# Loading the second chunk of w1 on ScalarE's DMA queue, and SyncE's loads in the order of the source

## The chip, the cores and the metric

The kernel runs on one core of one Trainium2 chip. The metric is device time in microseconds (us), the median of several executions of the same program. The engines are TensorE (PE; its weight loads are shown apart, as PEld), VectorE (DVE), ScalarE (ACT), GpSimd (POOL) and SyncE (SP). SP only issues DMAs; its queue is shown as SPq, that of ScalarE as ACTq.

## The reference, cut to what matters

Two branches are computed from the same input x (2048 rows of 448) and mixed with a gate of one number per row: a linear-attention block (A) and a two-layer network with a squared ReLU (B).

```python
x = A_x
g = _sigmoid((x * gate_w).sum(-1, keepdims=True))
a = _A_ref(x, A_wqkv, A_wo)              # linear attention, 16 heads
h = x @ w1 + b1                          # 448 -> 1792
r = where(h > 0, h, 0);  h = r * r
b = h @ w2 + b2                          # 1792 -> 448
return g * a + (1 - g) * b
```

The change touches only how the first pieces of x and w1 come into SBUF.

## The kernel before

All matmuls run on operands that are split into a high and a low part, so that three products of a pair (high by high, high by low, low by high) give the accuracy of 32 bits. `split_hi` writes the high part (on ACT, here), `split_lo` the low part, source minus high part, on DVE. The 448 columns of the contraction are cut into four chunks c = 0 to 3 of 128 rows (the last holds 64 columns twice). x is cut into four blocks of 512 rows; a chunk of a block is a tile of 128 by 512, 256 KB. w1 is cut into two halves h of 896 columns, each half into a part g = 0 of 512 and a part g = 1 of 384 columns.

The kernel begins with 14 small matmuls on a constant (line 177, tile `warm_ps`). Meanwhile SP issues the first loads. Chunk 0 of x and of w1 come together in two loads, `xwr`, each with half of the columns of both. Then come, in pairs, chunks 1, 2 and 3 of x (`xr`) and of w1 (`w1r`, from `in_w1a`), then b1, two tiles of w2, four of wk and the g = 1 part of w1. The loop over c at line 549 works on four groups of 128 columns of w1 (f = 0 to 3) at once, in four PSUM banks. For c = 0 it splits the two `xwr` tiles and multiplies the high parts in four matmuls of 256 columns (line 549), then come ten matmuls of 512 columns (line 229). For c = 1 and 2, ACT writes x's high part (`xh<-xr`) and w1's (`w<-w1r`), DVE x's low part (`xl<-xr,xh`) and w1's (`w<-w1r,w`), each in this order, and PE does twelve matmuls: for each f, w high by x high, w high by x low, w low by x high. For c = 3 there are eight. Then PE goes on to the keys (`k_ps`) and the second layer (`o_ps`).

The order on PE, ACT and DVE is that of the source: these three engines stand in the set that `manual_schedule` names (line 170). SP's order was up to a scheduler. A load into a tile of `work` waits until the tile that had its place is read; there are 15 places (`NSLOT`). Besides, the loads share eight completion semaphores in turn, so that one that takes a semaphore waits until the load that had it before has landed. `half` is a table of 128 by 2 that the queries of the last phase use.

Of the kernel before, what the change touches and what calls it, by code (L numbers as in the profile page):

```python
# [7 lines left out]
F = mybir.dt.float32  # L8
R = mybir.dt.float32r
AF = mybir.ActivationFunctionType  # L10
# [5 lines left out]
P = 128  # L16
# [14 lines left out]
def gated_mix_kernel(ctx: ExitStack, tc: tile.TileContext, xw, xt, xn, wk, wq, wv, wo, w1a, w1b, w2, b1, b2, gw,  # L31
                     hmask, kvmask, halves, out):
    nc = tc.nc
    act, dve, pool, pe, sp = nc.scalar, nc.vector, nc.gpsimd, nc.tensor, nc.sync
# [19 lines left out]
    def slot(shape, dt, name):  # L54
        return work.tile(shape, dt, name=name, tag="s", bufs=NSLOT)

    def load(dst, src):
        sp.dma_start(out=dst, in_=src)
# [45 lines left out]
    def load_x(b, c):  # L104
        x_raw[b, c] = slot([P, TB], F, f"xr{b}_{c}")
        load(x_raw[b, c], xt[b, c])
# [21 lines left out]

    w1_s, w1_raw = {}, {}

    def load_w1(h, g, c):
        w1_raw[h, g, c] = slot([P, (TB, 3 * P)[g]], F, f"w1r{h}{g}{c}")
        load(w1_raw[h, g, c], (w1a, w1b)[g][h, c])

    def new_w1(h, g):
        n, a, z = ((TB, 0, 16), (3 * P, 48, 0))[g]
# [30 lines left out]
        load(wk_raw[c], wk[c])  # L167


    ctx.enter_context(tc.manual_schedule(engines={pe.engine, act.engine, dve.engine}))  # L170


    part = [keep.tile([P, D], F, name=f"part{t}") for t in range(NT)]
# [13 lines left out]
        load(xw_raw[n], xw[n])  # L187
    for c in range(1, 4):
        load_x(0, c)
        load_w1(0, 0, c)  # L190
    b1_s = keep.tile([P, NF], F, name="b1_s")
    half = keep.tile([P, 2], F, name="half")
    ones = keep.tile([P, 2], F, name="ones")
    logit = keep.tile([P, NT], F, name="logit")
# [7 lines left out]
    for c in range(4):  # L202
        load_w1(0, 1, c)
# [415 lines left out]
    for b in range(1, NB):  # L619
        for f in range(NH):  # L620
# [46 lines left out]
            if b == 3:  # L667
                if f < 4:
                    load_w1(1, 0, f)
                if f == 4:  # L670
                    for c in range(4):
                        split_w1(1, 0, c)
                if f >= 2:
                    load_w2(NH + f - 2)
                if f >= 3:
                    split_w2(NH + f - 3)
                if f == 5:
                    key_sums()
                if f >= 5:
                    load_kv(2 * f - 10)  # L680
                    load_kv(2 * f - 9)
# [151 lines left out]
```

## Time and profile before

| | us |
|---|---|
| median of 3 runs | 435.24 (435.14 to 435.32) |
| profiled execution, its own time | 435.1 |
| its span, first to last instruction | 433.3 |
| PE busy | 429.0 |
| DVE busy | 284.2 |
| ACT busy | 174.6 |
| POOL busy | 72.0 |

Times in the views below are microseconds from the start of the span. PE is busy nearly always; what can be won or lost is in the stretches in which its weight loads wait. A busy PE counts a matmul's time in the pipeline, so two matmuls in a row overlap, and the pace is read from start to start.

### The profile page before, as it was taken

What the parts mean: (1) busy time and instruction counts of PE and PEld (TensorE: products, weight loads), DVE (VectorE), ACT (ScalarE), POOL (GpSimd) and SP (SyncE); (2) the same over time, 40 slices, a digit from 0 to 9 for tenths busy, and PEclk for the clock granted to TensorE, in tenths of its full rate; (3) what the DMA queues carried; (4) which work ended last, traced back from release to release, by engine and by line L of the source; (5) the groups of instructions that cost most, each with busy time, mean ns of one, the idle gap of its engine ahead of it and who ended that gap; (6) DMA issues with size and microseconds to landing.
All of it is one profiled execution on the core that took longest, in us unless ns stands there. A gap on an engine that the chain in (4) does not pass through costs nothing.

```text
span 433.3 us, 5562 instructions
## 1 busy us (share of the span) xinstructions
PE 429.0 (99%) x2052; PEld 380.6 (88%) x2052; DVE 284.2 (66%) x463; ACT 174.6 (40%) x302; POOL 72.0 (17%) x93
## 2 busy tenths in 40 slices
PE   9999999999999999999999999999999999999996
PEld 6889999898989899898898888988888888888986
DVE  5999518843499437884459777877654967457624
ACT  6865324521346132453145543444433534233421
POOL 0045006500065002540010441000100001000000
PEclk9999999999999999999999999999999999999999
DMA  8741302020232211223244321230101401002002
GB/s 277 246 134 61 99 0 69 26 67 2 70 85 65 70 45 48 66 57 111 63 117 146 72 63 38 63 120 0 26 0 48 137 0 27 0 0 86 0 2 85
DMA packets 18411, 29.11 MB, mean 67 GB/s; under 512 B 2896, under 2 KB 12736, under 8 KB 18384
## 3 DMA queue, kind: packets, MB, share of 16 engines
q1 hardware_dynamic: 16480, 26.46, 19.6%
q0 software_dynamic: 1760, 2.20, 2.3%
q8 instruction: 16, 0.26, 0.3%
q10 hardware_dynamic: 144, 0.10, 0.1%
q14 instruction: 11, 0.09, 0.1%
HBM read 22.43 MB, written 3.67 MB: 60 GB/s over the span
## 4 chain that ended last, share of the span: by engine, by line
PE 98%; DMA 1%; DVE 0%; ACT 0%; DVEq 0%; issue 0%
PE h_ps L229 32%; PE o_ps L254 31%; PE q_ps L84 8%; PE a_ps L84 8%; PE g_ps L84 8%; PE k_ps L254 8%; PE kv_ps L405 1%; DMA xwr<-in_xw 1%; PE m_ps L84 1%; PE d_ps L84 0%; PE h_ps L549 0%; PE z_ps L399 0%; DVE out L278 0%; ACT xh L65 0%; DVEq L829 0%
## 5 line engine op out<-in xcount | busy, mean ns | idle before, releaser
L254 PE MATMUL o_ps<-w,hh 128*128 128x448 f32 x448 | 129.0, 362 | 0.0
L229 PE MATMUL h_ps<-xh,w 128*128 128x512 f32 x390 | 124.7, 390 | 0.0
L254 PEld LDWEIGHTS o_ps<-w,hh 128*128 128x128 f32 x448 | 84.0, 187 | 7.7
L229 PE MATMUL h_ps<-xl,w 128*128 128x512 f32 x224 | 86.7, 389 | 0.0
L229 PEld LDWEIGHTS h_ps<-xh,w 128*128 128x128 f32 x390 | 73.1, 188 | 14.8 <-DVE w L72 0.4
L254 PE MATMUL o_ps<-w,hl 128*128 128x448 f32 x224 | 81.2, 362 | 0.0
L233 ACT ACTIVATE hr<-h_ps,b_s 128x512 f32<-128x512 f32 x56 | 38.1, 680 | 85.9 <-PE h_ps L229 80.6
L69 DVE CAST hh<-hr 128x512 fp32r<-128x512 f32 x56 | 23.6, 421 | 61.4 <-ACT hr L234 61.3
L229 PEld LDWEIGHTS h_ps<-xl,w 128*128 128x128 f32 x224 | 42.0, 188 | 7.8
L254 PEld LDWEIGHTS o_ps<-w,hl 128*128 128x128 f32 x224 | 42.0, 188 | 3.7
L72 DVE TENSOR_TENSOR hl<-hr,hh 128x512 fp32r<-128x512 f32 x56 | 39.7, 709 | 3.3
L72 POOL TENSOR_TENSOR nl<-xnr,nh 128x384 fp32r<-128x384 f32 x16 | 17.2, 1075 | 119.0 <-ACT nh L65 118.9
L234 ACT ACTIVATE hr<-hr 128x512 f32<-128x512 f32 x56 | 35.4, 632 | 1.8
L84 PE MATMUL q_ps<-xh,wq_s 128*128 128x512 f32 x100 | 33.0, 389 | 0.0
L84 PE MATMUL a_ps<-m_s,qh 128*128 128x448 f32 x112 | 32.7, 362 | 0.0
L254 PE MATMUL k_ps<-wk_s,xh 128*128 128x448 f32 x112 | 32.7, 361 | 0.0
L476 POOL DMA_DIRECT2D qr<-qv x16 | 7.9, 500 | 124.3 <-ACT qv L473 94.4
L72 DVE TENSOR_TENSOR pl<-r,ph 128x448 fp32r<-128x448 f32 x16 | 23.7, 1480 | 0.0
L327 POOL TENSOR_TENSOR ksum<-ksum,r 128x448 f32<-128x448 f32 x15 | 23.3, 1555 | 1.1 <-DVE r L289 1.1
L84 PE MATMUL q_ps<-xl,wq_s 128*128 128x512 f32 x60 | 23.3, 389 | 0.0
L254 PE MATMUL k_ps<-wk_s,xl 128*128 128x448 f32 x64 | 23.2, 363 | 0.0
L84 PE MATMUL a_ps<-m_s,ql 128*128 128x448 f32 x64 | 23.2, 362 | 0.0
(112 smaller groups left out, 565.9 us busy)
## 6 DMA issues: line engine op xcount, KB each, us to landing
xr<-in_xt SPq DMA_DIRECT2D x27, 256.0 KB, 2.7
xnr<-in_xn SPq DMA_DIRECT2D x16, 224.0 KB, 2.5
out<-out SPq DMA_DIRECT2D x15, 224.0 KB, 1.9
w2r<-in_w SPq DMA_DIRECT2D x14, 224.0 KB, 2.8
w1r<-in_w1a SPq DMA_DIRECT2D x7, 256.0 KB, 2.8
w1r<-in_w1b SPq DMA_DIRECT2D x8, 192.0 KB, 3.3
m_s<-m POOLq DMA_DIRECT2D x12, 112.0 KB, 2.5
wqr<-in_wq SPq DMA_DIRECT2D x4, 256.0 KB, 2.6
```

What stands on the lines that cost most here:

```text
L69: eng.tensor_copy(hi, src)
L72: eng.tensor_tensor(lo, src, f32(hi), op=ALU.subtract)
L84: pe.matmul(out_ps, a, b, start=(i == 0), stop=(i == n - 1))
L229: pe.matmul(ps, a, m, start=(c == 0 and n == 0), stop=(c == 3 and n == 1))
L233: act.activation(r, ps, AF.Relu, bias=b1_s[:, f:f + 1])
L234: act.activation(r, r, AF.Square)
L254: pe.matmul(ps, a, m, start=start, stop=stop)
L327: pool.tensor_tensor(ksum, ksum, p, op=ALU.add)
L405: pe.matmul(kv_ps[:JE, js], wv_s[c][:, js], gsum[c][:, js], start=(c == 0), stop=(c == 3))
L476: pool.dma_start(out=r[p + 16:p + 32], in_=v[p:p + 16])
```

## The change

`load_w1` gets a queue as an argument. For chunk 1 of the first part of w1 it is ACT's: ACT first writes a constant into one column of the destination tile, and then issues the load, which has to come behind that write. The table of functions that ACT loads before its first activation thereby stands before the load. A second small activation writes a column of `b1_s`, so that SP's load of b1 has to come behind it. SP joins the engines whose order is the source's. The loads of x's chunk 1 and chunk 2 now follow each other on SP, and chunk 2 of w1 comes behind them. The load of `half` goes from behind b2 to the place that it has in the source.

```diff
-    def load_w1(h, g, c):
+    def load_w1(h, g, c, queue=sp):
         w1_raw[h, g, c] = slot([P, (TB, 3 * P)[g]], F, f"w1r{h}{g}{c}")
-        load(w1_raw[h, g, c], (w1a, w1b)[g][h, c])
+        if queue is act:
+            act.activation(w1_raw[h, g, c][:, :1], nc.const_aps.tensor(1.0, (P, 1), F), AF.Copy)
+        queue.dma_start(out=w1_raw[h, g, c], in_=(w1a, w1b)[g][h, c])
...
-    ctx.enter_context(tc.manual_schedule(engines={pe.engine, act.engine, dve.engine}))
+    ctx.enter_context(tc.manual_schedule(engines={pe.engine, act.engine, dve.engine, sp.engine}))
...
     for c in range(1, 4):
         load_x(0, c)
-        load_w1(0, 0, c)
+        if c > 1:
+            load_w1(0, 0, c)
+
+
     b1_s = keep.tile([P, NF], F, name="b1_s")
+    load_w1(0, 0, 1, act)
+    act.activation(b1_s[:, :1], nc.const_aps.tensor(1.0, (P, 1), F), AF.Copy)
```

SP at the program's start, before (`xr0_1` is chunk 1 of x's block 0, `w1r001` is chunk 1 of w1's half 0, part 0; the last number only counts tiles):

```order
L58 DMA xwr0_110<-in_xw 128x512
L58 DMA xwr1_112<-in_xw 128x512
L58 DMA xr0_1_114<-in_xt 128x512
L58 DMA w1r001_116<-in_w1a 128x512
L58 DMA xr0_2_118<-in_xt 128x512
L58 DMA w1r002_120<-in_w1a 128x512
L58 DMA xr0_3_122<-in_xt 128x512
L58 DMA w1r003_124<-in_w1a 128x512
L58 DMA b1_s_126<-in_b1 128x14
```

and after:

```order
L58 DMA xwr0_110<-in_xw 128x512
L58 DMA xwr1_112<-in_xw 128x512
L58 DMA xr0_1_114<-in_xt 128x512
L58 DMA xr0_2_116<-in_xt 128x512
L135 DMA w1r002_118<-in_w1a 128x512
L58 DMA xr0_3_120<-in_xt 128x512
L135 DMA w1r003_122<-in_w1a 128x512
L58 DMA b1_s_124<-in_b1 128x14
```

The load of `w1r001` has left SP's queue, and each load behind it stands one place earlier.

ACT at the program's start, before:

```order
L65 ACT_TABLE_LOAD
L65 ACTIVATE xh0_169<-xwr0_110 128x256
L65 ACTIVATE xh0_169<-xwr1_112 128x256
L65 ACTIVATE xh0_169<-xr0_1_114 128x512
L65 ACTIVATE w1_00_171<-w1r001_116 128x512
L65 ACTIVATE xh0_169<-xr0_2_118 128x512
```

and after:

```order
L134 ACT_TABLE_LOAD
L134 ACTIVATE w1r001_125<-const-float32-1.0 128x1
L135 DMA w1r001_125<-in_w1a 128x512
L198 ACTIVATE b1_s_124<-const-float32-1.0 128x1
L65 ACTIVATE xh0_171<-xwr0_110 128x256
L65 ACTIVATE xh0_171<-xwr1_112 128x256
L65 ACTIVATE xh0_171<-xr0_1_114 128x512
L65 ACTIVATE w1_00_173<-w1r001_125 128x512
L65 ACTIVATE xh0_171<-xr0_2_116 128x512
```

Three instructions stand between the table load and the first high part; the order of the high parts themselves is as before. On PE, DVE and POOL nothing has moved.

## Rows read from the trace of the kernel before

**Rows 1.** The page: span, and busy time of each engine.

```profile
span 433.3 us, 5562 instructions
...
PE 429.0 (99%) x2052; PEld 380.6 (88%) x2052; DVE 284.2 (66%) x463; ACT 174.6 (40%) x302; POOL 72.0 (17%) x93
```

**Rows 2.** Waits of weight loads, whole span: total us, times, longest.

```profile
PEld h_ps L549 <- ACT xh L65: 0.6, 1, 0.6
PEld h_ps L229 <- DVE w L72: 0.4, 1, 0.4
PEld h_ps L229 <- ACT w L65: 0.4, 1, 0.4
```

**Rows 3.** Timeline of PE's start, from several windows: start, us, instruction, count.

```profile
0.78 3.15 PE L177 MATMUL warm_ps<-const-bfloat16-1.0 128*128 128x256 bf16 x14 [0.78 <-PEq L825]
4.01 1.21 PE L549 MATMUL h_ps<-xh,w 128*128 128x256 f32 x4
...
4.63 0.59 PE L549 MATMUL h_ps<-xh,w 128*128 128x256 f32 x2
...
6.45 1.08 PE L229 MATMUL h_ps<-xh,w 128*128 128x512 f32 x4
...
8.77 0.40 PE L229 MATMUL h_ps<-xl,w 128*128 128x512 f32 x1
9.00 0.62 PE L229 MATMUL h_ps<-xh,w 128*128 128x512 f32 x2
...
9.69 0.62 PE L229 MATMUL h_ps<-xh,w 128*128 128x512 f32 x2
```

**Rows 4.** Timeline of weight loads, 6.9 to 9 us; in brackets, idle time before.

```profile
7.47 0.19 PEld L229 LDWEIGHTS h_ps<-xh,w 128*128 128x128 f32 x1 [0.36 <-ACT w L65]
...
8.19 0.30 PEld L229 LDWEIGHTS h_ps<-xh,w 128*128 128x128 f32 x2 [0.43 <-DVE w L72]
```

**Rows 5.** Timeline of ACT's start.

```profile
0.74 1.28 ACT L65 ACT_TABLE_LOAD   x1 [0.74 <-PEq L825]
...
4.16 0.42 ACT L65 ACTIVATE xh<-xwr 128x256 fp32r<-128x256 f32 x1 [0.20 <-DMA xwr<-in_xw]
5.87 0.63 ACT L65 ACTIVATE xh<-xr 128x512 fp32r<-128x512 f32 x1 [1.29 <-DMA xr<-in_xt]
6.78 0.63 ACT L65 ACTIVATE w<-w1r 128x512 fp32r<-128x512 f32 x1 [0.28 <-DMA w1r<-in_w1a]
7.46 0.63 ACT L65 ACTIVATE xh<-xr 128x512 fp32r<-128x512 f32 x1
...
13.99 0.69 ACT L233 ACTIVATE hr<-h_ps,b_s 128x512 f32<-128x512 f32 x1 [0.38 <-PE h_ps L229]
```

**Rows 6.** Timeline of DVE, 3 to 9 us.

```profile
6.54 0.69 DVE L72 TENSOR_TENSOR xl<-xr,xh 128x512 fp32r<-128x512 f32 x1 [0.74 <-ACT xh L65]
7.45 0.69 DVE L72 TENSOR_TENSOR w<-w1r,w 128x512 fp32r<-128x512 f32 x1 [0.22 <-ACT w L65]
```

**Rows 7.** Timeline of SP's start: when it issues a DMA, and how long.

```profile
0.74 0.86 SPq L58 DMA_DIRECT2D xwr<-in_xw  x2
1.64 0.43 SPq L58 DMA_DIRECT2D xr<-in_xt  x1
2.12 0.43 SPq L58 DMA_DIRECT2D w1r<-in_w1a  x1
```

**Rows 8.** DMA issues at 1.6 and 2.1 us: count, KB, us from issue to landing.

```profile
xr<-in_xt SPq DMA_DIRECT2D x1, 256.0 KB, 4.2
...
w1r<-in_w1a SPq DMA_DIRECT2D x1, 256.0 KB, 4.6
```

**Rows 9.** Windows: busy of PE, PEld, DVE, ACT, POOL; PEclk, DMA share, GB/s.

```profile
2.50:4.50 2.00, 1.91 (x9) 1.18 (x7) 0.64 (x3) 0.76 (x2) 0.00 (x0) 1.00 1.01 369
4.50:7.50 3.00, 3.00 (x15) 2.17 (x14) 2.04 (x6) 1.39 (x4) 0.00 (x0) 1.00 0.99 293
```

**Rows 10.** The smallest activation (by line), and `half`'s first reader (by tile).

```profile
L380 ACT ACTIVATE gate<-logit 128x16 f32<-128x16 f32 x1 | 0.2, 199 | 0.0
...
L77 ACT ACTIVATE ql<-qe,half x4: 723/724/726, 271.5 to 407.3; 128x512 fp32r<-128x512 f32 x4
```

## Prediction

> **What bounds the kernel now.** I first read the busy times on the page [rows 1]: PE is busy 429.0 of 433.3 us, so only its own waits, or its own pace, can move the end. Then the waits of its weight loads over the whole span [rows 2]: apart from 0.7 us before the first warm-up matmul there are three, 0.6, 0.4 and 0.4 us, and the timelines put all three ahead of 8.2 us [rows 3, 4]. After that the loads never starve PE. So the change, which moves only loads at the start, can at most remove what lies there, and a delay made there goes straight to the end, since nothing later is idle to take it up.
>
> The first wait (PE's first real matmul at 4.01) hangs on `xwr`, whose two issues the change leaves first on SP. The other two are chunk 1. The ten 512-column matmuls of chunk 0 end with four that start from 6.45 on [rows 3]. The pace of such matmuls without waits is 0.23 us: three start between 9.00 and 9.69. So the next was due at 6.45 + 4 x 0.23 = 7.37. It came at 7.47, released by ACT's high part of w1 [rows 4], and the third at 8.19, released by DVE's low part of w1. Behind each wait the next matmul comes 0.33 us later rather than 0.23. Follow it to the fifth matmul of chunk 1, which starts at 8.77 [rows 3] and would be due at 7.37 + 4 x 0.23 = 8.29: chunk 1 costs 0.48 us of waiting. **This is the most that the change can win.** 0.2% of this kernel, about what a measurement can tell from no change, is 0.87 us.
>
> **How chunk 1 comes to its times.** x's chunk 1 is issued at 1.64 and lands 4.2 us later, w1's at 2.12 and 4.6 us later [rows 7, 8], thus at 5.84 and 6.72. ACT starts on them at 5.87 and 6.78, 0.63 us each, and DVE follows [rows 5, 6]: x's low part 6.54 to 7.23, w1's 7.45 to 8.14. For other landings I use these spacings: if ACT starts x's high part at X, and w1 is ready for ACT at W, the high part of w1 starts at the later of X + 0.65 and W; DVE's low part of w1 starts 0.67 later (not before X + 1.36, where x's low part ends), takes 0.69, and the third matmul comes 0.06 later. The fifth is 0.57 after a third that had to wait. With X = 5.87 and W = 6.78 this gives 8.20 and 8.77, as the rows have it.
>
> **The change part by part.**
> *ACT's queue.* The table load ends at 0.74 + 1.28 = 2.02 [rows 5]. The added one-column activation is bounded by zero and by the smallest activation in the trace, 0.199 us for 16 columns [rows 10]; I take 0.2, as most of such a short one is fixed. ACT then issues the load at about 2.25, with SP's 0.43 us for an issue [rows 7], and a second 0.2 us follows: ACT is free at 2.9, and it waits for `xwr` until 3.55 anyhow. So the two activations and the issue cost nothing, but **the load is issued no earlier than before** (2.25 against 2.12). Its first packets reach the DMA engines about as late as before.
> *SP's queue.* It is one issue shorter, so x's chunk 2 goes out at 2.12 and each later load 0.47 us earlier. That is worth something only if issuing held the transfers back. It doesn't: from 2.5 to 7.5 us the DMA engines are busy 1.01 and 0.99 [rows 9], and loads are issued every 0.47 us while chunks 1 of x and w1 land 0.88 apart. I count zero; nothing later waits on PE's side that an earlier chunk 2 could free.
> *What shares the engines.* 256 KB at the 293 to 369 GB/s of these windows [rows 9] take 0.7 to 0.9 us. Before, the loads came one after the other out of one queue. Now w1's chunk 1 stands in a second queue and reaches the engines at a time (before the second `xwr` is in at 4.16 on the slowest of them [rows 5]) when x's chunk 1 is still queued in the first. Both queues draw on the same bandwidth and the bytes needed for chunk 1 are the same, so the later of the two lands near 6.7 as before. What can change is the earlier one. ACT's order still wants x first, and an x that comes later costs more than a w1 that comes earlier brings. The ends: x as before and w1 early gives X = 5.87, W below 6.52: third matmul at 7.98, fifth at 8.55, so -0.22; both early enough gives the full -0.48. x in w1's old place, X = 6.78, gives a third at 8.85 and a fifth at 9.42: +0.65. If the two share evenly, I put both half-way between the old landings, X = W = 6.33: w1's high part at 6.98, its low part 7.65 to 8.34, third 8.40, fifth 8.97: **+0.20**. I take this value, since the start of the new load (about 3.2, if it needs as long from issue as the first `xwr` did to its first share) lies ahead of x's chunk 1 in the queue on some engines and behind it on others.
> *xwr itself.* If the new packets go ahead of the second `xwr` on an engine that lags, that tile is up to 0.7 us late. Its pair of matmuls then goes from 4.63 [rows 3] to 5.3, and the ten that follow end some 0.47 later, with chunk 1 due at 7.84. Its fifth is then due at 8.76, as it came before: by itself this hides in the waits of chunk 1.
> *b1, half and the rest.* b1 now waits for ACT's second small write at 2.9, before SP reaches it; its first reader comes at 13.99 [rows 5]. `half` is issued later, in the middle phase, and is first read at 271.5 [rows 10]. Both cost nothing. The later loads keep their sequence.
>
> Sum: 0 + 0 + 0.20 + 0 us against the profiled execution of 435.1 (433.3 span and 1.8 around it), which is 0.14 under the median; on the median, 435.24 + 0.20 = 435.44.
>
> **The rivals.**
> (1) *Nothing moves.* The change doesn't do what it says: the second queue brings the load no earlier, x keeps its place. For it: issue at 2.25 against 2.12, DMA engines full [rows 9]. Time 435.24. The Trainium skill, "DMA: Bandwidth & Descriptors", section "Issuing engines are not separate DMA queues", says that issuing from several engines saves only the issuing engine's time; full DMA engines in these rows agree, and by it the sum would be 0.
> (2) *w1 comes early and x on time.* For it: at 5.87 and 6.78 ACT waits for DMA only [rows 5], and 293 GB/s in this stretch against 369 just before [rows 9] leaves room that a second queue might fill. Against: the engines show no idle share. -0.22 to -0.48, 434.76 to 435.02.
> (3) *x and w1 change places*, or w1 falls behind x's chunk 2, which was in by 7.46 [rows 5]: X = 6.78 gives +0.65; W = 7.46 gives w1's low part 8.13 to 8.82 and a fifth at 9.45, +0.68. 435.89 to 435.92. The Trainium skill, same page, section "Queues, rings and completion order", says that each DMA engine goes round its queues and drains a whole packet of several descriptors before it turns. By that rule the new load's share goes ahead of x's chunk 1 on most engines, and the time would be this rival's 435.89; no row here shows two queues loaded at once.
> (4) *The clock rises later: slower.* The 14 warm-up matmuls of 256 columns come every 0.21 us or so (3.15 us in all), the pace of 1.2 GHz, while 512 columns later take 0.23, that of 2.4 GHz [rows 3]; so TensorE begins at its lower level though the clock column reads 1.00 throughout. It comes up about the second pair at 4.63, after an almost unbroken row of matmuls. A late second `xwr` would open a gap just there. If the rise then missed chunk 0, its ten matmuls would cost 0.23 more each: +2.3, 437.5. It decides from a second `xwr` that is several tenths late and a pair that is shown at the slow pace after 5 us. Against: the row of work before it is the same as now.
>
> **How the numbers follow.** Forecast, shared engines, 435.44 (itself 435.2 to 435.7): 0.35. Nothing moves: 0.20. Early w1: 0.20. Changed places: 0.16. Late clock: 0.05. Mishaps that I can't name, both signs: 0.04. The range reaches from the full gain, 434.76, to the changed places, 435.92, widened by the scatter of 0.1 seen between runs: 434.7 to 436.0; it leaves out the late clock and the mishaps. All but these lie within 0.87 us of the old time: same 0.89; slower 0.08 (late clock, and changed places together with a late `xwr`); faster 0.03, as no mechanism here gives more than 0.48.
>
> **What would show it.** In the profile after: ACT's small activation and issue between 2.0 and 2.9; x's chunk 1 read by ACT later than 5.87 and w1's no later than 7.0; weight loads of chunk 1 waiting about 0.6 to 0.7 in all; the second pair of line 549 near 4.63; no wait after 9 us. I am wrong if ACT starts x's chunk 1 at 5.87 or before with w1 right behind it (rival 2), if one of them starts after 6.7 (rival 3), if 512-column matmuls after 5 us come at twice 0.23 (rival 4), or if a load wait appears later in the span, which I count at nothing.

## The result, and the profile after

The changed kernel takes 436.10 us in the median (435.46 to 436.97, 22 runs) against 435.25 of the kernel before beside it (434.66 to 435.76, 22 runs): 0.85 us more, a ratio of 1.0020 with a 95% interval of 1.0014 to 1.0026. The profiled execution took 435.83, with a span of 434.1 against 433.3 [rows 1].

The waits of the weight loads over the whole span, as in [rows 2]:

```profile
PEld h_ps L236 <- ACT w L65: 1.3, 1, 1.3
PEld L179 <- issue: 0.8, 1, 0.8
PEld h_ps L556 <- ACT xh L65: 0.7, 2, 0.4
PEld h_ps L236 <- DVE w L72: 0.4, 1, 0.4
```

The wait for ACT's high part of w1 has grown from 0.4 to 1.3 us; nothing waits that did not wait before. The timeline of PE's start, to lay beside [rows 3]:

```profile
0.78 2.97 PE L179 MATMUL warm_ps<-const-bfloat16-1.0 128*128 128x256 bf16 x14 [0.78 <-PEq L832]
3.89 1.11 PE L556 MATMUL h_ps<-xh,w 128*128 128x256 f32 x4
...
6.22 1.07 PE L236 MATMUL h_ps<-xh,w 128*128 128x512 f32 x4
8.16 0.50 PE L236 MATMUL h_ps<-xh,w 128*128 128x512 f32 x1 [0.88 <-ACT w L65]
8.50 0.39 PE L236 MATMUL h_ps<-xl,w 128*128 128x512 f32 x1
8.97 0.73 PE L236 MATMUL h_ps<-xh,w 128*128 128x512 f32 x2
9.54 0.39 PE L236 MATMUL h_ps<-xl,w 128*128 128x512 f32 x1
```

Chunk 0 ends earlier than before (its last four start from 6.22, not 6.45), but chunk 1 begins at 8.16 instead of 7.47, and its fifth matmul at 9.54 instead of 8.77. That is 0.77 us, of 0.8 us in the span: the whole loss lies ahead of 9.6 us. The timeline of ACT, with its queue, beside [rows 5]:

```profile
0.74 1.28 ACT L134 ACT_TABLE_LOAD   x1 [0.74 <-PEq L832]
2.03 0.20 ACT L134 ACTIVATE w1r<-const-float32-1.0 128x1 f32<-128x1 f32 x1
2.26 0.38 ACTq L135 DMA_DIRECT2D w1r<-in_w1a  x1
2.69 0.20 ACT L198 ACTIVATE b_s<-const-float32-1.0 128x1 f32<-128x1 f32 x1 [0.46 <-ACT w1r L134]
3.42 0.42 ACT L65 ACTIVATE xh<-xwr 128x256 fp32r<-128x256 f32 x1 [0.52 <-DMA xwr<-in_xw]
...
6.96 0.63 ACT L65 ACTIVATE xh<-xr 128x512 fp32r<-128x512 f32 x1 [2.52 <-DMA xr<-in_xt]
7.50 0.61 ACT L65 ACTIVATE w<-w1r 128x512 fp32r<-128x512 f32 x1
8.02 0.62 ACT L65 ACTIVATE xh<-xr 128x512 fp32r<-128x512 f32 x1
```

The three added instructions are over at 2.9 and delay nothing. But x's chunk 1 is there at 6.96 instead of 5.87, and w1's no longer makes ACT wait, since it is read right behind. The landings, as in [rows 8], of DMAs issued at 1.64 and, on ACT's queue, at 2.26:

```profile
xr<-in_xt SPq DMA_DIRECT2D x1, 256.0 KB, 5.3
```

```profile
w1r<-in_w1a ACTq DMA_DIRECT2D x1, 256.0 KB, 5.1
```

So x lands at 6.94 and w1 at 7.36, against 5.84 and 6.72 before. **Both loads of chunk 1 have become late, not one for the other's sake.** Packets by queue, q1 being SP's and q10 ACT's, from 2.3 to 4.25 us, from 4.25 to 5.25 and from 5.25 to 6.9 (queue, kind: packets, MB, share of the 16 engines):

```profile
q1 hardware_dynamic: 355, 0.66, 102.6%
```

```profile
q1 hardware_dynamic: 68, 0.12, 52.8%
q10 hardware_dynamic: 22, 0.05, 18.6%
```

```profile
q1 hardware_dynamic: 193, 0.35, 57.7%
q10 hardware_dynamic: 121, 0.22, 43.3%
```

ACT's load gets no packet before 4.25, some 2 us after its issue. Then it shares the engines with what stands on SP's queue, at first with a small part, and from 5.25 on with 43.3% of their time against 57.7%.

### The profile page after: what moved, and what is told of

Same layout as the page of the kernel before. It is cut to its first block, busy times and chain, and to the rows that moved or that the text cites. A ratio compares the mean times of both kernels' runs of the same rounds, so it can differ in the third digit from the quotient of the medians.

```text
span 434.1 us, 5563 instructions
## 1 busy us (share of the span) xinstructions
PE 428.6 (99%) x2052; PEld 380.4 (88%) x2052; DVE 284.0 (65%) x463; ACT 174.7 (40%) x304; POOL 72.1 (17%) x93
## 4 chain that ended last, share of the span: by engine, by line
PE 97%; DMA 1%; DVE 0%; issue 0%; SPq 0%; ACT 0%; DVEq 0%
PE h_ps L236 32%; PE o_ps L261 31%; PE q_ps L84 8%; PE a_ps L84 8%; PE k_ps L261 8%; PE g_ps L84 8%; DMA xr<-in_xt 1%; PE kv_ps L412 1%; PE m_ps L84 1%; PE d_ps L84 0%; SPq L58 0%; PE z_ps L406 0%; DVE w L72 0%; ACT xh L65 0%; DVE out L285 0%
```

## The experiments

All are built from the changed kernel and were timed beside the kernel before, 7 to 12 runs each. Each pair of times is a pair of medians; the ratio behind it, with its 95% interval, is estimated from all executions and is not the quotient of the two medians. The diffs are cut to the lines that matter, with loops written out. w1_1 is chunk 1 of w1, x2 chunk 2 of x, and so on. Unless a diff says otherwise, the small activations stay, and SP's order is the source's.

**One queue again.**

```diff
     for c in range(1, 4):
         load_x(0, c)
-        if c > 1:
-            load_w1(0, 0, c)
+        load_w1(0, 0, c)
-    load_w1(0, 0, 1, act)
-    act.activation(b1_s[:, :1], ...)
+    for i in range(2):
+        act.activation(b1_s[:, i:i + 1], ...)
```

> The changed kernel with w1's chunk 1 back on SP in its old place (x1, w1_1, x2, w1_2, ...); SyncE in the source's order and the two small activations of ACT stay (both write b1's tile). Theory A (what is lost comes from the pair of chunk 1 sharing the DMA engines with x's chunk 2 and landing late): ACT starts x's chunk 1 near 5.9 and w1's near 6.8, fifth matmul of chunk 1 near 8.8, median 435.25 +- 0.2. Rival B (SP's order over the rest of the kernel, or the small activations, cost the time): median near 436.1.

435.15 against 435.34, ratio 0.9998 (0.9989 to 1.0006). The rival falls: SP's order over the rest of the kernel and the small activations cost nothing that these runs can tell. The waits were not as expected: in the profiled execution (435.31) x1 is read at 6.38 and w1_1 at 7.03, and the fifth matmul starts at 9.01, later than the 5.9, 6.8 and 8.8 of theory A.

**The order alone, on one queue.** SP issues x1, x2, w1_1, w1_2, x3, w1_3.

```diff
-        if c > 1:
-            load_w1(0, 0, c)
+    load_x(0, 1); load_x(0, 2); load_w1(0, 0, 1); load_w1(0, 0, 2); load_x(0, 3); load_w1(0, 0, 3)
```

> One queue, but SP issues x1, x2, w1_1, w1_2, x3, w1_3: the order in which the changed kernel's loads leave, without a second queue. Theory A1 (the order alone does it, x2 ahead of w1_1): x1 is on time near 5.9, w1_1 lands near 7.4, fifth matmul near 9.45, median near 435.9 to 436.1. Rival A2 (two queues in flight together slow all of them): x1 and w1_1 both land in turn and the loss is below 0.4, median below 435.7.

435.67 against 435.34, ratio 1.0010 (1.0002 to 1.0019): a loss, but less than either the changed kernel's 0.85 or the 0.68 of the arithmetic. The expectation that the order alone does it (435.9 to 436.1) missed. The pair was run again, beside the changed kernel on the same chip:

> One queue with x2 ahead of w1_1, the same kernel as in the first set, beside the changed kernel on the same chip. If the order alone makes the loss, the two agree within 0.2 us; if the second queue adds to it, as the first set says (+0.33 against +0.85), this one is 0.3 to 0.6 faster.

> The changed kernel as it is, for the comparison on one chip with the single-queue run in the same order of loads. Its first measurement says 436.1, +0.85.

435.63 for the order alone (1.0010, 1.0001 to 1.0019) and 436.11 for the changed kernel (1.0021, 1.0012 to 1.0030), against 435.14. Two sets agree: the order costs 0.3 to 0.5 us, and the second queue about 0.5 more (on one chip, in the second set, 0.48 by the medians and 0.37 by the means, give or take 0.28). The repeat's profile shows the order's part on ACT:

```profile
5.84 0.63 ACT L65 ACTIVATE xh<-xr 128x512 fp32r<-128x512 f32 x1 [1.32 <-DMA xr<-in_xt]
7.34 0.63 ACT L65 ACTIVATE w<-w1r 128x512 fp32r<-128x512 f32 x1 [0.87 <-DMA w1r<-in_w1a]
```

x1 is on time as in [rows 5]; w1_1, now behind x2, starts at 7.34 instead of 6.78.

**Two queues, or one, with nothing behind the pair.** x2 and all loads behind it on SP wait for a small activation that writes a column of x2's tile, behind ACT's first high part.

```diff
+    def held_loads():
+        x_raw[0, 2] = slot([P, TB], F, "xr0_2")
+        act.activation(x_raw[0, 2][:, :1], ...)          # called behind split_hi of xwr0
+        load(x_raw[0, 2], xt[0, 2])
+        ...                                              # then w1_2, x3, w1_3, b1, w2, wk, w1b
```

> The changed kernel, but x's chunk 2 and all loads behind it on SP are held back until ACT has written the first half of x's chunk 0 (near 4.2 us), so that x1 on SP and w1_1 on ACT have the DMA engines to themselves. Theory A1 (x2's bytes ahead of the pair): the pair lands by 6.3, waits of chunk 1 under 0.3, median 434.8 to 435.3. Rival A2 (a second queue that starts while the first is full stalls the engines by itself): x1 still later than 6.5, median 435.7 to 436.1.

> One queue with the old order x1, w1_1, and x2 and all behind it held back to about 4.2 us as in the run with two queues. If loads that are in flight behind the pair slow it (theory A1 in its strong form), the pair lands earlier than before, ACT starts x1 before 5.6 and the median is 434.8 to 435.1. If a queue serves its loads in turn and those behind cost nothing: 435.25 +- 0.2, or later if chunk 2 now comes late for ACT (after 8 us).

Two queues: 435.34 against 435.34 (0.9999, 0.9990 to 1.0008). The loss of the changed kernel is gone with w1_1 still on ACT's queue, so most of it hangs on what goes along with w1_1 on SP. The first expectation's time holds, its waits don't: x1 was read at 6.39 here, and chunk 1 still waited. One queue: 434.99 (0.9988, 0.9979 to 0.9997). That the second queue costs nothing by itself is therefore not shown: held in the same way and timed in the same set, one queue is faster than two by 0.35 in the medians and 0.30 in the means, give or take 0.26. ACT's first reads of chunk 1, with two queues and with one:

```profile
6.39 0.63 ACT L65 ACTIVATE xh<-xr 128x512 fp32r<-128x512 f32 x1 [1.58 <-DMA xr<-in_xt]
6.93 0.62 ACT L65 ACTIVATE w<-w1r 128x512 fp32r<-128x512 f32 x1
```

```profile
5.80 0.63 ACT L65 ACTIVATE xh<-xr 128x512 fp32r<-128x512 f32 x1 [1.00 <-DMA xr<-in_xt]
6.49 0.63 ACT L65 ACTIVATE w<-w1r 128x512 fp32r<-128x512 f32 x1
```

With nothing else let in, x1 is read 0.59 later in the execution in which w1_1 shares the engines with it. The one queue, held, repeated:

> The held single queue of the first set again, the only version so far that was under the kernel before (434.99 against 435.34). If that was real: 434.8 to 435.1 with the kernel before near 435.25. If chance, equal within 0.1.

435.18 against 435.20 (0.9997, 0.9989 to 1.0006): the gain was not there again. The repeat's profile suggests why so little is left, though its chunk 1 waits for nothing. The waits of its weight loads, and ACT's rows:

```profile
PEld h_ps L562 <- ACT xh L65: 0.5, 1, 0.5
PEld o_ps L265 <- DVE r L299: 0.3, 1, 0.3
PEld o_ps L265 <- DVE hl L72: 0.2, 1, 0.2
```

```profile
6.42 0.63 ACT L65 ACTIVATE w<-w1r 128x512 fp32r<-128x512 f32 x1
8.56 0.63 ACT L65 ACTIVATE xh<-xr 128x512 fp32r<-128x512 f32 x1 [1.51 <-DMA xr<-in_xt]
```

Holding x2 back makes ACT wait 1.5 us for it, all of ACT's and DVE's later splits come later, and the second layer (`o_ps`) waits in their place. A shorter hold, a one-column copy on POOL as soon as the first `xwr` is in:

> One queue in the old order with x2 and all behind it held back only until the first xwr has landed (a one-column copy on POOL, near 3.6 us, instead of 4.4 in the run with the ACT hold). Theory A (fewer loads in flight let the pair of chunk 1 land earlier): the pair as early as in that run, and the later waits for chunk 2 and the second layer's loads, seen there, smaller: median 434.7 to 435.0. Rival (the gain of that run was chance): 435.2 to 435.4.

435.03 against 435.14 (1.0000, 0.9991 to 1.0008): no difference that these runs can tell, with one execution of 11 at 436.60.

**Which load behind the pair matters.** First x2 at once, w1_2 and all behind it held; then w1_2 in x2's place with nothing held.

```diff
     load_x(0, 1)
     load_x(0, 2)
     load_w1(0, 0, 1, act)
+    # w1_2, x3, ... wait for a small activation behind xwr0's high part
```

> The changed kernel with x2 going out at once, ahead of the pair as changed, but w1_2 and all behind it on SP held back to about 4.4 us. If x2 alone takes the pair's bandwidth, the loss stays: median 435.9 to 436.2. If the second queue's extra loss (436.1 against 435.65 on one queue) comes from the loads behind x2, which on one queue would have to wait for the pair and on two queues do not: 435.4 to 435.7.

435.49 against 435.20 (1.0010, 1.0001 to 1.0018). With only x2 beside the pair, two queues cost 0.29, about what the order alone costs on one queue; the other 0.5 or so of the changed kernel comes with the loads behind x2. The steps are taken from different sets, each against its own kernel before.

```diff
     load_x(0, 1)
+    load_w1(0, 0, 2)
     load_x(0, 2)
     load_x(0, 3)
+    load_w1(0, 0, 3)
```

> The changed kernel with SP's loads in the order x1, w1_2, x2, x3, w1_3; w1_1 on ACT as changed. If w1_1 loses because whatever stands behind x1 on SP takes turns with it: as the changed kernel, 435.8 to 436.3. If x2 as such matters (ACT wants x before w): 435.2 to 435.6.

436.37 against 435.11 (1.0030, 1.0016 to 1.0044; 7 runs, 435.61 to 437.98). Not x2 as such: with w1_2 in its place the loss is there as well, and not to be told from the changed kernel's. On one queue the loads behind w1_1 wait for it; in a queue of its own w1_1 has no place ahead of them.

**ACT issues w1_1 at once**, ahead of its table load, at 0.74 instead of 2.26.

```diff
-    load_w1(0, 0, 1, act)
+    act.dma_start(out=w1_raw[0, 0, 1], in_=w1a[0, 1])
```

> The changed kernel, but ACT issues w1_1 at once, near 0.74, ahead of its table load, instead of at 2.26; all else as changed. Theory Q (part of the loss is that the second queue's load starts only after what the first queue already holds, its first packets 2.0 us after its issue): w1_1 is in before 5.5, its wait is gone, xwr may come some tenths later; median 435.2 to 435.7. Rival (two queues in flight slow each other whenever they start): as the changed kernel or worse, 436.0 or more.

Four executions at 435.35 to 435.50, eight at 437.06 to 437.58; median 437.27 against 435.14. In the profiled one, of the lower group, chunk 1 waits for nothing, but the first `xwr` is read at 4.30 instead of 3.55 and PE stands still for 0.85 us meanwhile. The upper group lies 1.9 us higher. To see whether that is the clock, PE's gap was filled:

```diff
-    for _ in range(14):
+    for _ in range(18):
         pe.matmul(warm_ps[:, :256], warm[:, :P], warm, start=True, stop=True)
```

> The run in which ACT issued w1_1 first gave 435.4 in some executions and 437.3 in others; its xwr landed at 4.3, and PE had nothing to do from 3.7 to 4.8. Here 18 warm-up matmuls instead of 14 fill that gap (to 4.6). If the upper group is TensorE staying at its lower clock because of the gap: no execution above 436.2, median 435.2 to 435.6. If it is anything in the DMAs: the upper group near 437.3 stays.

Ten of twelve executions at 435.43 to 435.70, two at 437.3 and 437.5. The upper group shrinks from eight to two. Neither outcome of the expectation came, and the two runs were made on different chips (12 and 14), so that the gap feeds the group is not shown by this pair; a pair on one chip follows below. The kernel before has such executions too, two of 170 (437.13 and 437.50). No execution of an upper group was profiled in these two kernels. Of the granted clock there is only the mean of each execution: 1.00 in nine of the ten, 0.996 in the one at 437.30. A fall to half for some 3 us would lower that mean to 0.996, so nine of them had none; a late rise would not show in it, as the column also reads 1.00 while the matmuls still go at the slow pace (last section). What sets the upper groups stays open. A fall of the clock is shown in the run with w1_2 first, whose profiled execution took 437.98, with a mean granted clock of 0.996. Its windows (busy of PE, PEld, DVE, ACT, POOL; PEclk, DMA share, GB/s) and PE's timeline:

```profile
7.10:8.70 1.60, 0.17 (x1) 0.00 (x0) 0.69 (x1) 1.23 (x3) 0.00 (x0) 1.00 1.02 377
...
10.60:13.90 3.30, 3.30 (x9) 2.59 (x8) 3.20 (x7) 2.91 (x6) 0.00 (x0) 0.50 0.92 292
14.00:15.00 1.00, 1.00 (x6) 0.84 (x5) 1.00 (x3) 0.58 (x1) 0.00 (x0) 1.00 1.03 381
```

```profile
8.78 0.50 PE L237 MATMUL h_ps<-xh,w 128*128 128x512 f32 x1 [1.51 <-ACT w L65]
...
10.96 0.63 PE L237 MATMUL h_ps<-xl,w 128*128 128x512 f32 x1
11.39 1.05 PE L237 MATMUL h_ps<-xh,w 128*128 128x512 f32 x2
12.24 0.63 PE L237 MATMUL h_ps<-xl,w 128*128 128x512 f32 x1
```

PE was busy 0.17 of 1.60 us while chunk 1 was late; then, from 10.6 to 13.9, the granted clock is 0.50, 1.2 GHz, and 512-column matmuls come every 0.43 us instead of 0.23. Eight matmuls at 0.20 more each are 1.6 us, which is what this execution took above the run's median of 436.37: if the wait brought the fall about, as their order suggests, the wait of 1.5 us was paid for twice. That is one execution; no other profiled one shows a fall there.

**The second queue where its load is needed together with SP's**: the second `xwr` on ACT at once, SP with x1, w1_1, x2, ... as before, each one place further ahead.

```diff
-        load(xw_raw[n], xw[n])
+        (sp, act)[n].dma_start(out=xw_raw[n], in_=xw[n])
```

> The second queue used for the second xwr at once (0.74, ahead of ACT's table load), all else in the old order on SP. If a second queue is harmless where both of its neighbours are needed at the same time: first matmul some tenths later, second pair earlier, x1 and w1_1 as before or earlier, median 435.0 to 435.4. If the two queues slow each other, both xwr land after 4.2 and some runs show the late clock (437 and more), as in the run where ACT issued w1_1 first.

> The second xwr on ACT's queue at once, old order on SP, again. If the gain was real (x1 lands near 4.7 instead of 5.8, so chunk 1 waits for nothing): 434.6 to 434.9, ratio clearly under 1. If chance: 435.1 to 435.3.

First set, on chip 14: 434.79 against 435.20 (0.9995, 0.9986 to 1.0004), no execution above 435.50. Second set, on chip 5: six executions at 434.60 to 435.35 and six at 436.48 to 437.13, all of these with a mean granted clock of 1.00, median 435.92 against 435.11. PE's gap ahead of its first real matmul is 0.41 us in both profiles. Filling it, with 16 warm-up matmuls:

> As the run before it, with 16 warm-up matmuls instead of 14, so that PE is busy to 4.2 until its first real matmul near 4.3. If the late clock in some executions comes from that gap: the upper executions near 435.5 go, median 434.5 to 434.8. If not: no change within 0.1.

> Second xwr on ACT's queue, 16 warm-up matmuls, again. If the gain is real: 434.7 to 435.0 against 435.2, no execution above 436. If chance: equal within 0.1.

434.90 against 435.11 (0.9991, 0.9980 to 1.0002) and 434.87 against 435.30 (0.9991, 0.9982 to 1.0000): no execution of 22 above 435.69, 0.2 to 0.4 us under the kernel before, each interval just reaching no change. The first of the two was made on chip 5 beside the six upper executions of the unfilled kernel, so there it is the filling that goes with their absence. ACT and PE in the first of these:

```profile
4.81 0.63 ACT L65 ACTIVATE xh<-xr 128x512 fp32r<-128x512 f32 x1 [0.20 <-DMA xr<-in_xt]
6.05 0.63 ACT L65 ACTIVATE w<-w1r 128x512 fp32r<-128x512 f32 x1 [0.61 <-DMA w1r<-in_w1a]
```

```profile
0.78 3.57 PE L179 MATMUL warm_ps<-const-bfloat16-1.0 128*128 128x256 bf16 x16 [0.78 <-PEq L829]
4.35 1.22 PE L553 MATMUL h_ps<-xh,w 128*128 128x256 f32 x4
...
6.89 1.30 PE L233 MATMUL h_ps<-xh,w 128*128 128x512 f32 x5
8.02 0.39 PE L233 MATMUL h_ps<-xl,w 128*128 128x512 f32 x1
8.25 0.62 PE L233 MATMUL h_ps<-xh,w 128*128 128x512 f32 x2
8.70 0.39 PE L233 MATMUL h_ps<-xl,w 128*128 128x512 f32 x1
```

x1 is read at 4.81, 1.06 us before the kernel before, w1_1 0.73 before, and PE goes through chunk 1 without a stop (fifth matmul 8.70 against 8.77, after a first pair that started 0.34 later). One warm-up matmul more:

> One more warm-up matmul (17), which ends near 4.35, about when the first pair is due. If the gap in the warm-up is what matters: as the run with 16 or 0.1 faster. If the warm-up now delays the first pair: 0.1 to 0.2 slower than with 16.

435.09 against 435.30 (0.9996, 0.9987 to 1.0005), not to be told from 16.

## Why the prediction was wrong

The place was right and the size was not. The direction of its sum was also right, +0.20, but 0.85 was measured, just beyond the range's end of 436.0.

- *What bounds the kernel, and where the change acts:* held. The loss is in the waits of chunk 1, and no other wait appeared. The single queue in the old order costs nothing that can be told, so nothing later in the kernel takes part.
- *ACT's queue:* held: activation 0.20, issue at 2.26 and 0.38 long instead of 0.43, free at 2.9. The load was issued no earlier than before.
- *b1, `half`, later order:* held, by the same run.
- *SP's queue, counted at zero:* **this step failed.** I asked what the 0.47 us earlier issue was worth and found nothing, but x2 had not only become earlier, it had moved ahead of w1_1. On one queue that alone costs 0.3 to 0.5 us. I had this as half of rival 3 only ("w1 falls behind x's chunk 2", +0.68), and left it out of the sum.
- *What shares the engines:* **failed by its premise** that the bytes needed for chunk 1 are the same and the later of the two lands near 6.7. That holds only if nothing else is let in. Other loads of SP, x2 and w1_2 among them, were served while w1_1 and the tail of x1 were under way, with 57.7% of the engines' time from 5.25 on: X was 6.96 and W 7.36 or so, not 6.33 for both. With all of them held, the sharing came out much as I had put it (x1 read at 6.39, w1_1 right behind at 6.93). The held runs (no change with all held, +0.29 with x2 free, +0.85 with nothing held) show these loads' share. Put X = 6.96 into the prediction's own spacings: x's low part ends at 8.32, the fifth matmul starts at 9.64, +0.87; it started at 9.54, +0.77, as DVE began w1's low part at 8.23. The spacings were right within 0.1; the landings were wrong.
- *A slip of 0.04 in the sum:* for X = W = 6.33, and for X = 6.78, I let w1's low part start before x's low part ends, against my own rule (not before X + 1.36). By the rule the sum is +0.24 and the changed places +0.69. That changes nothing here.
- *Rival 1* fell: x didn't keep its place. *Rival 2* fell for this change; a second queue with which x1 does come earlier is seen in the runs with the second `xwr` on ACT, where x1 stands one place further ahead on SP. *Rival 3* came nearest, and its sign (a start after 6.7) is what the profile showed; it took x late or w1 late, where both were, so its 435.92 lies 0.18 us under the result and the range's end 0.1. The rule of the Trainium skill that I set beside it ("DMA: Bandwidth & Descriptors", section "Queues, rings and completion order": each DMA engine goes round its queues) agrees with this trace as to turns: from 5.25 on the two queues had 57.7 and 43.3% of the engines' time. That the new load's share would go ahead of x1 on most engines, as I read from it, it didn't: 355 packets of SP's queue moved from 2.3 to 4.25 us and none of ACT's. The other rule of the Trainium skill, that issuing from several engines saves only the issuing engine's time (same page, section "Issuing engines are not separate DMA queues"), would have left the time as it was; the measured 0.5 us or so between one queue and two in the same order goes against that, since the second queue also changed who waits for whom. *Rival 4* did not make this result: chunk 0 ended 0.23 us earlier than before. In the repeat of the changed kernel the slow pace lasted longer (its first two 512-column matmuls start 0.42 us apart, and chunk 0's last four from 6.94), yet that execution took 435.54, the least of its 11. The fall of the clock with w1_2 first is another thing, a fall after a wait and not a late rise.
- The chance of 0.08 for slower by over 0.2% looks too low for the same reason, though the time came out at the very edge of it: 0.85 us is 0.195% of 435.25, and the interval reaches to 0.26%.

What stays open: how much of the changed kernel's loss is x1's lateness and how much w1_1's. In the profiled execution x1 set it, as w1_1 was in at 7.36, before ACT turned to it at 7.50. Landings of a single profiled execution scatter: x1 was read between 5.84 and 6.62 in the two profiles of one and the same single-queue kernel. Still, in the seven profiles with all loads in one queue x1 was read at 5.78 to 6.62, and at 6.68, 6.96 and 7.27 in the three with w1_1 on ACT's queue from 2.26 on and nothing held. No view tells the packets of one load from those of another on the same queue, so how SP's later loads came ahead of x1's last packets is argued and not shown. A slump of DMA rate that the changed kernel's trace shows from 4.0 to 5.5 us (195 GB/s) looked like a cause at first. The repeat of that kernel had 268, and the single queue in the old order 242 at the old time, so it isn't one.

## What to carry to other kernels

Where the DMA engines are full, ask of every moved load which loads it goes ahead of and which it now shares with, and not only when it is issued. Here the place in one queue was also a priority: on a queue of its own, w1_1 lost its place ahead of the loads that SP issued behind it. In the one place where the second queue's load was needed at the same moment as the first queue's, it perhaps brought 0.2 to 0.4 us, with a warm-up that reached up to the first real matmul; without that, half of the executions of one set came out some 2 us slower. In one execution a transfer that came late at the start was followed by a lower clock of TensorE and cost about twice its wait, so look at single executions, not at the median alone.

## What the runs showed of the hardware

The first packet of ACT's load came some 2 us after its issue in the changed kernel (2.26 to past 4.25; 4.4 in the repeat). SP's first packet came about 1.0 after its issue at 0.74, and ACT's 1.3 to 1.6 after an issue at 0.74, in the seven traces of kernels in which ACT issues at once. So the later issue met a longer delay. That x2 and the loads behind it made the delay is not shown: with all of them held, ACT's first packet still came at 4.1. TensorE's pace at the start is not the same in every execution, while the clock column reads 1.00 in all of them there: in the run with the shorter hold the first 512-column matmuls took

```profile
5.15 1.05 PE L241 MATMUL h_ps<-xh,w 128*128 128x512 f32 x2
6.00 1.29 PE L241 MATMUL h_ps<-xl,w 128*128 128x512 f32 x4
7.13 1.32 PE L241 MATMUL h_ps<-xh,w 128*128 128x512 f32 x5
```

that is, 0.43 us each for the first two (5.15 to 6.00), the pace of 1.2 GHz, and 0.23 from the last row on. In that execution the pace, and no load, set chunk 1: none of its weight loads waits, and its fifth matmul still starts at 8.98. So where two limits end near the same time, an earlier landing can leave the other to set the end.
